# Four of the last ten stores in three parts of 112, 8 and 8 rows

## The chip, the core and the metric

The kernel runs on one core of one Trainium2 chip. The metric is the device time of one execution in microseconds, and the number for a kernel is the median of several executions. Times inside an execution come from a hardware profile of one further execution; they count from its first instruction.

The engines of the core are named as the profile names them: PE (TensorE, matmul), PEld (its weight loads), DVE (VectorE), ACT (ScalarE), POOL (GpSimd) and SP (SyncE). Sixteen DMA engines move data between the device's memory (DRAM) and the on-chip memory (SBUF, 128 partitions, called rows here). A DMA instruction on SP's or POOL's queue only starts a transfer; the DMA engines carry it out.

## What is computed

An input of 8 sequences, 3264 positions and 192 channels first passes a depthwise convolution over the last seven positions with softmax weights for each of 8 heads. The result x then passes a spectral mix: its lowest 64 Fourier modes along the sequence are multiplied by one complex 192 x 192 matrix for each mode, transformed back and added, and a last product with a relu follows.

```python
x = attn_out                        # the convolution's result
X = np.fft.rfft(x, axis=1)
Xr, Xi = (np.real(X[:, :n_modes]), np.imag(X[:, :n_modes]))
Yr = np.einsum('bmd,mde->bme', Xr, w_r) - np.einsum('bmd,mde->bme', Xi, w_i)
Yi = np.einsum('bmd,mde->bme', Xr, w_i) + np.einsum('bmd,mde->bme', Xi, w_r)
Y[:, :n_modes] = Yr + 1j * Yi
y = np.fft.irfft(Y, n=S, axis=1)
u = x + y
return (u + np.maximum(u @ w_ch, 0.0)).astype(np.float32)
```

The output is float32 in DRAM, 8 x 3264 x 192, 20 MB.

## The kernel before

The kernel works in two long stages. In the first (to about 97 us) POOL's queue loads x and the mode matrices, and PE convolves, transforms and mixes. In the second (from about 105 us to the end) the output is computed and stored, item by item. This second stage is what the change touches.

**Items.** The 8 sequences are taken as four pairs (NQ = 4, index q). A sequence is cut into 13 blocks of 256 positions (NB = 13), the last one of 192. One item is one block of one pair: the list `duos` (line 669) has N = 52 of them, n = 0 to 51. Partition p of an item holds two neighbouring positions (index a) of each of the two sequences (index i), so an item is 128 partitions x 2 x 2 x 192 float32 values, 384 KB. Items 12, 25, 38 and 51 are the short last blocks of a pair: they have 96 partitions (PL) and 288 KB.

**The computation of an item.** For each a, PE forms the sum in one bank of its accumulator memory with `product` (line 722) and `full` (line 702), ACT applies the relu in place (`clamp`, line 695), and `add` (line 673) lets DVE add x and write the result to an output buffer in SBUF (line 684). Only the very last half item is copied by ACT (line 682), after PE has added x with the identity matrix (line 803). There are NO = 6 output buffers, called arena in the profile; item n uses buffer n % 6.

**The stores.** After the second half (a = 1) of an item, `add` starts one DMA on SP's queue that writes the whole item to DRAM (line 690). The first three items are stored in two halves. For each partition the DMA moves two runs, one for each sequence of the pair; each run is 2 x 192 float32 values, 1536 bytes. A store of 128 rows is thus 256 packets of 1536 bytes, and one of 96 rows 192. There are 55 stores in all, and SP does nothing else in this stage. SP issues them in the order of the items: before each it waits for DVE's result, and, in an EVENT_SEMAPHORE instruction of the same line, for the completion of an earlier DMA, since the stores take turns on eight completion semaphores. At the end (line 896) SP waits for all of them.

**The order of the work around it.** The loop at line 839 runs over the half items k and mixes the products of neighbouring half items by hand, so that PE always has something to do; the last six half items (TAIL) have an order of their own. The change leaves all of this as it is.

Of the kernel before, what the change touches and what calls it, by code (L numbers as in the profile page):

```python
# [20 lines left out]
def kernel(  # L21
# [9 lines left out]
    nc = tc.nc  # L31
    B, S, D = x.shape
# [5 lines left out]
    P = 128  # L38
# [120 lines left out]
    def load_part(q, b0, n):  # L159
# [6 lines left out]
        if nf < n:  # L166
# [6 lines left out]
                                           ap=[[0, P], [KK, H], [1, KK]]))  # L173
# [64 lines left out]
    for h0 in (0, H // 2):  # L238
        hs = slice(h0, h0 + H // 2)
        for lag in range(KK):  # L240
            k = lag // 2
            nc.vector.copy_predicated(
                out=pk4[:, hs, lag % 2, :],
                mask=masks[:, PW * k:PW * (k + 1)].unsqueeze(1).to_broadcast([P, H // 2, PW]),
                data=ta3[:, hs, KK - 1 - lag:KK - lag].to_broadcast([P, H // 2, PW]))
        for g in range(4):
            c0 = 1 + 32 * (g % 2)
            dst, srcv = band[32 * g:32 * g + 32, hs, :, c0:c0 + PW], pk4[32 * g:32 * g + 32, hs, :, :]
# [421 lines left out]
    N = len(duos)  # L670
    place = {}

    def add(bank, n, a):

        o = outs[n % NO]
        q, t = duos[n][0]
        pn = PL if t == NT - 2 else P
        s = NT * q + t
        srcv = bank[0:pn, 0:2 * D].rearrange("p (i d) -> p i d", i=2)
        if (n, a) == (N - 1, 1):  # L680

            nc.scalar.copy(out=o[0:pn, :, a, :], in_=srcv)  # L682
        else:
            nc.vector.tensor_tensor(out=o[0:pn, :, a, :], in0=srcv, in1=xall[0:pn, s + a, :, :], op=ALU.add)  # L684
        apart = n < 3
        if apart or a == 1:
            a0, w = (a, 1) if apart else (0, 2)
            dst = bass.AP(tensor=out.tensor, offset=out.offset + (2 * q * S + P * t + a0) * D,
                          ap=[[2 * D, pn], [S * D, 2], [1, w * D]])
            nc.sync.dma_start(out=dst, in_=o[0:pn, :, a0:a0 + w, :].rearrange("p i a d -> p i (a d)"))  # L690

    def clamp(bank, on_scalar=True):
        z = bank[:, 0:2 * D]
# [57 lines left out]
    d = ND - 2  # L751
# [12 lines left out]
    d = ND - 1  # L764
# [25 lines left out]
    def upper_y(k):  # L790
        if 0 <= k < K - 2:
            turn([end[k, 0]])
            product(k, 1, pieces(k, 1, "y")[0], False, True)
            add(bank[k], *items[k])

    def lower_y(k):
        if 0 <= k < K - 2:
            product(k, 0, pieces(k, 0, "y")[0], False, False)
        elif K - 2 <= k < K:
            n, a = items[k]  # L800
            if k == K - 1:
                qt = NT * duos[n][0][0] + duos[n][0][1] + a
                nc.tensor.matmul(bank[k][:, 0:2 * D], ident[:], xall[:, qt, :, :].rearrange("p i d -> p (i d)"),  # L803
                                 start=False, stop=False, skip_group_check=True)
            full(n, "y", a)
            add(bank[k], n, a)
# [10 lines left out]
    for n in range(2):  # L817
        whole(n, "y")
        for a in range(2):
            add(place[n][a], n, a)  # L820
# [80 lines left out]
```

## Time and profile before

| what | value |
|---|---|
| median of 3 runs | 171.35 us (171.32 to 171.36) |
| time of the profiled execution | 171.73 us |
| its span, from the first to the last instruction | 169.9 us (169.87) |
| granted TensorE clock, mean | 0.999 |
| stores: DMA issues on SP of line 690 | 55 |
| bytes written to DRAM | 20.05 MB |
| DMA queue q1 (SP's), packets | 14848 |
| DMA queue q8 (instruction), packets and bytes | 20, 0.33 MB |

The span is what the engines' instructions cover; the time of an execution also has what lies around it, 1.9 us here. Busy time says how long an engine worked, in total; the 40 slices show when. A slice of this span is 4.25 us. The views used below are the page (busy times, slices, DMA issues), the chain of waits that ended last, stages (a row gives the stage, then for PE, PEld, DVE, ACT and POOL the busy time with the number of instructions, then the granted PE clock, the busy share of the DMA engines and GB/s), and the instructions of one line (duration as min/median/max in ns, first and last start). The trace also lists every DMA packet with its start, duration and size, and the time of each completion, but not the DMA engine that carried it.

### The profile page before, as it was taken

The page shows a single profiled execution, that of the slowest core. Times are in us where ns is not written, and L with a number is a line of the kernel's source. Part 1 is how long each engine was busy: PE and PEld are TensorE (multiplying, and loading weights), DVE is VectorE, ACT ScalarE, POOL GpSimd, SP SyncE. Part 2 cuts the span into 40 slices and gives each one's busy share as a digit, 9 for nine tenths or more (in the row PEclk, how much of TensorE's full clock was granted, in tenths as well). Part 3 has the DMA queues.
Part 4 walks back from the last instruction along what each step waited for, and adds up shares of the span by engine and source line. Part 5 has one row for each costly group of instructions (what it writes and reads, how often), then busy time and mean ns, then how long its engine had stood idle before and what let it go on. Part 6 is the DMA issues. An engine that isn't in the chain of part 4 may idle for free.

```text
span 169.9 us, 6328 instructions
## 1 busy us (share of the span) xinstructions
PE 159.1 (94%) x2643; PEld 126.9 (75%) x2643; DVE 125.2 (74%) x245; ACT 109.9 (65%) x209; POOL 38.7 (23%) x71
## 2 busy tenths in 40 slices
PE   6997789999999999999999998999999999999980
PEld 6983666776565655579999865899999999999940
DVE  4899554684572845748778644899999999999990
ACT  8485870653572735636776753788888888887770
POOL 7941763341521712002620000600000000000000
PEclk9999999999999999999999999999999999999999
DMA  2999999999999999999999970589899999999995
GB/s 26 193 202 204 204 204 204 203 204 203 202 204 204 207 208 208 208 207 208 211 203 208 209 126 4 170 310 357 305 350 359 346 320 344 351 326 340 339 387 173
DMA packets 37180, 40.09 MB, mean 236 GB/s; under 512 B 1984, under 2 KB 37152, under 8 KB 37152
## 3 DMA queue, kind: packets, MB, share of 16 engines
q0 software_dynamic: 22304, 19.61, 71.9%
q1 hardware_dynamic: 14848, 20.09, 32.4%
q8 instruction: 20, 0.33, 0.8%
q14 instruction: 8, 0.07, 0.1%
HBM read 39.10 MB, written 20.05 MB: 348 GB/s over the span
## 4 chain that ended last, share of the span: by engine, by line
DMA 58%; PE 36%; issue 1%; POOL 1%; ACT 1%; POOLq 0%; ACTq 0%
PE z L722 34%; DMA xall<-in_x_dram 25%; DMA arena<-in_moe_w_i_dram 18%; DMA ct<-in_moe_w_i_dram 14%; POOL xall L165 1%; PE z L702 1%; PE z L643 0%; PE z L551 0%; ACT z L695 0%; ACT arena L682 0%; PE z L634 0%; ACT shared L569 0%; PE z L644 0%; PE z L575 0%; PE z L803 0%
## 5 line engine op out<-in xcount | busy, mean ns | idle before, releaser
L684 DVE TENSOR_TENSOR arena<-z,xall 128x384 f32<-128x384 f32 (+1 forms) x103 | 56.7, 557 | 2.1 <-PE z L722 0.6
L695 ACT ACTIVATE z<-z 128x384 f32<-128x384 f32 x102 | 48.0, 475 | 11.1 <-PE z L722 2.7
L722 PE MATMUL z<-wm,ct 64*128 64x192 bf16 x200 | 47.4, 243 | 0.0
L722 PE MATMUL z<-arena,ftab 64*128 64x384 bf16 x308 | 44.5, 322 | 0.0
L722 PEld LDWEIGHTS <-ct 64*128 64x128 bf16 x600 | 38.5, 94 | 4.7 <-issue 0.3
L317 PE MATMUL z<-xall,shared 64*64 64x480 bf16 (+3 forms) x768 | 38.5, 338 | 2.2 <-DMA xall<-in_x_dram 1.5
L317 PEld LDWEIGHTS <-shared 64*64 64x64 bf16 x768 | 25.1, 106 | 13.3 <-DMA xall<-in_x_dram 1.6
L722 PE MATMUL z<-wsw,ct 64*128 64x192 bf16 x300 | 34.0, 243 | 0.0
L722 PEld LDWEIGHTS <-ftab 64*128 64x128 bf16 x396 | 33.4, 94 | 0.6 <-issue 0.3
L361 DVE CAST xall<-z 128x480 bf16<-128x480 f32 (+1 forms) x32 | 20.6, 645 | 12.7 <-PE z L317 11.7
L359 ACT CAST xall<-z 128x480 bf16<-128x480 f32 (+1 forms) x32 | 17.5, 548 | 15.2 <-PE z L317 15.2
L722 PE MATMUL z<-w,ct 64*128 64x192 bf16 x100 | 24.3, 243 | 0.0
L416 DVE COPY ct<-z 128x1024 bf16<-128x1024 bf16 x27 | 18.4, 687 | 5.2 <-PE z L419 4.5
L419 PE MATMUL z<-ident,xall 128*128 128x128 bf16 x312 | 20.0, 219 | 0.0
L419 PEld LDWEIGHTS <-xall 128*128 128x128 bf16 x312 | 17.7, 98 | 1.9 <-issue 1.1
L378 PE MATMUL z<-xall,ftab 128*128 128x384 bf16 (+3 forms) x114 | 18.0, 312 | 0.2 <-DVE xall L361 0.2
L165 POOL DMA_DIRECT2D xall<-in_x_dram x16 | 14.2, 894 | 12.8 <-DMA xall<-in_x_dram 11.9
L378 PEld LDWEIGHTS <-ftab 128*128 128x128 bf16 (+1 forms) x114 | 10.2, 98 | 7.6 <-issue 1.5
L414 ACT COPY ct<-z 128x1024 bf16<-128x1024 bf16 x12 | 12.1, 1012 | 4.1 <-PE z L419 4.1
L722 PE MATMUL z<-mixa,ftab 64*128 64x384 bf16 x88 | 13.4, 323 | 0.0
L196 PE MATMUL z<-xall 128*128 128x144 bf16 x92 | 7.9, 264 | 1.6 <-DVE xall L183 1.6
L296 POOL DMA_DIRECT2D arena<-in_moe_w_r_dram x7 | 4.6, 652 | 20.6 <-PE z L551 14.5
(116 smaller groups left out, 140.6 us busy)
## 6 DMA issues: line engine op xcount, KB each, us to landing
out_dram<-arena SPq DMA_DIRECT2D x45, 384.0 KB, 3.5
xall<-in_x_dram POOLq DMA_DIRECT2D x4, 864.0 KB, 17.4
xall<-in_x_dram POOLq DMA_DIRECT2D x4, 576.0 KB, 18.7
arena<-in_moe_w_r_dram POOLq DMA_DIRECT2D x3, 576.0 KB, 15.0
arena<-in_moe_w_i_dram POOLq DMA_DIRECT2D x3, 576.0 KB, 14.8
ct<-in_moe_w_r_dram POOLq DMA_DIRECT2D x3, 576.0 KB, 20.6
ct<-in_moe_w_i_dram POOLq DMA_DIRECT2D x3, 576.0 KB, 23.6
xall<-in_x_dram POOLq DMA_DIRECT2D x2, 672.0 KB, 11.4
```

Source lines behind the costliest of these rows:

```text
L165: nc.gpsimd.dma_start(out=xin[:, s0:s0 + nf, 2 * D * i:2 * D * (i + 1)], in_=src)
L196: nc.tensor.matmul(free[3][:, 0, 0:144], zeros[:, 0:P], zeros[:, 0:144], start=True, stop=True, skip_group_check=True)
L317: yield nc.tensor.matmul(o, band[r, h, int(a != a1), c0:c0 + 64], xin5[r, s1:s1 + n, :, a1, dsl], start=(row == 0 and a1 == 0), stop=(row ...
L359: nc.scalar.copy(out=dst[:, a], in_=srcv)
L361: nc.vector.tensor_copy(out=dst[:, a], in_=srcv)
L378: nc.tensor.matmul(xp[:, :, ds], ftab[0:k, t, :], xall[0:k, NT * q + t, :, ds], start=(j == 0), stop=(j == len(work) - 1), skip_group_chec ...
L414: nc.scalar.copy(out=out, in_=in_)
L416: nc.vector.tensor_copy(out=out, in_=in_)
L419: nc.tensor.matmul(o, in_, ident[:], start=True, stop=True, is_transpose=True)
L684: nc.vector.tensor_tensor(out=o[0:pn, :, a, :], in0=srcv, in1=xall[0:pn, s + a, :, :], op=ALU.add)
L695: nc.scalar.activation(out=z, in_=z, func=ACT.Relu)
L722: mm = nc.tensor.matmul(target(bank[k], cols, r), l, r, start=first, stop=last, skip_group_check=True)
```

## The change

The stores of items N - 10, N - 8, N - 6 and N - 4, which are items 42, 44, 46 and 48, go in three DMAs instead of one: rows 0 to 111, rows 112 to 119 and rows 120 to 127. The bytes, their place in DRAM and the moment at which `add` starts them stay the same. All other items are stored in one DMA, as before.

```diff
+    PARTS, UNEVEN = (P - 16, 8, 8), (N - 10, N - 8, N - 6, N - 4)
+
     def add(bank, n, a):
...
         if apart or a == 1:
             a0, w = (a, 1) if apart else (0, 2)
-            dst = bass.AP(tensor=out.tensor, offset=out.offset + (2 * q * S + P * t + a0) * D,
-                          ap=[[2 * D, pn], [S * D, 2], [1, w * D]])
-            nc.sync.dma_start(out=dst, in_=o[0:pn, :, a0:a0 + w, :].rearrange("p i a d -> p i (a d)"))
+            p0 = 0
+            for rows in PARTS if n in UNEVEN else (pn,):
+                dst = bass.AP(tensor=out.tensor, offset=out.offset + (2 * q * S + P * t + a0 + 2 * p0) * D,
+                              ap=[[2 * D, rows], [S * D, 2], [1, w * D]])
+                nc.sync.dma_start(out=dst, in_=o[p0:p0 + rows, :, a0:a0 + w, :].rearrange("p i a d -> p i (a d)"))
+                p0 += rows
```

## The prediction

> **What bounds the kernel now.** I read the page first, for which engine is full where.
>
> ```profile
> PE 159.1 (94%) x2643; PEld 126.9 (75%) x2643; DVE 125.2 (74%) x245; ACT 109.9 (65%) x209; POOL 38.7 (23%) x71
> ...
> DMA  2999999999999999999999970589899999999995
> GB/s 26 193 202 204 204 204 204 203 204 203 202 204 204 207 208 208 208 207 208 211 203 208 209 126 4 170 310 357 305 350 359 346 320 344 351 326 340 339 387 173
> ```
>
> The last 60 us pair a PE that is full with DMA engines that are nearly full (310 to 387 GB/s, all of it the stores). Second, the chain of waits, for where compute ends.
>
> ```profile
> 164.63 0.32 PE z L803
> 164.96 0.18 PE z L702
> 165.13 0.02 issue
> 165.16 0.47 ACT arena L682
> ```
>
> Compute ends at 165.63, the span at 169.87. The 4.2 us between belong to stores alone, so third, the stages around the end.
>
> ```profile
> 152.40:153.40 1.00, 1.00 (x22) 0.96 (x20) 0.97 (x3) 0.90 (x2) 0.00 (x0) 1.00 0.94 270
> 155.00:156.00 1.00, 1.00 (x22) 0.92 (x20) 0.97 (x2) 0.81 (x3) 0.00 (x0) 1.00 0.94 350
> 161.00:162.00 1.00, 1.00 (x22) 0.85 (x19) 1.00 (x3) 0.77 (x3) 0.00 (x0) 1.00 1.04 389
> ...
> 166.80:167.50 0.70, 0.00 (x0) 0.00 (x0) 0.00 (x0) 0.00 (x0) 0.00 (x0) 1.00 1.00 290
> 168.00:168.60 0.60, 0.00 (x0) 0.00 (x0) 0.00 (x0) 0.00 (x0) 0.00 (x0) 1.00 0.06 23
> ```
>
> The last two numbers are the DMA share of 16 engines and GB/s. From 168.00 to 168.60 the share is 0.06, one engine of sixteen: 23 GB/s over 0.6 us is 14 KB, nine pieces of 1536 B. Fifteen engines are done, one is late by about 0.6 us, and the end waits for it. The trace's list of packets says the same: the latest engine's last packet ends at 168.60, the next one's at 167.98, and 1.27 us after 168.60 the span ends (landing, SP's last wait, the closing drains). That engine has been late since about 113 us. The page's queue q8 (instruction, 20 packets, 0.33 MB) explains it if they all pass through one engine: 0.8% of 16 spans of 169.9 us over 20 is 1.1 us each. A late engine works through a store in 0.97 us (landings of successive stores) and gets one each 1.145 us, so it recovers slowly.
>
> The second thing in these rows is the time of a packet: share x 16 us over the number of packets. At 155 it is 0.94 x 16 / (350,000/1536) = 66 ns, at 161 also 66. At 152.4 and 166.8, where the trace moves a 96-row store, it is 86 and 85 ns. A 96-row store gives an engine 12 packets instead of 16 and yet is hardly faster:
>
> ```profile
> out_dram<-arena SPq DMA_DIRECT2D x45, 384.0 KB, 3.5
> ...
> out_dram<-arena SPq DMA_DIRECT2D x4, 288.0 KB, 3.4
> ```
>
> [...]
>
> Fourth, SP, which issues every store.
>
> ```profile
> L690 SPq DMA_DIRECT2D out_dram<-arena x55: 334/372/769, 107.2 to 165.7; - x55
> L690 SPq EVENT_SEMAPHORE  x52: 17/17/727, 96.7 to 165.3; - x52
> ...
> DMA to landing us min/median/max: 2.0/3.4/4.4
> ```
>
> **The change, part by part.** Items 42, 44, 46 and 48 are touched (N is 52), issued at 156.09, 158.37, 160.66 and 162.62. No byte is added: 256 packets become 224 + 16 + 16.
>
> Issues: 8 more on SP. The nearest back-to-back issues, items 0 and 1, stand 0.46 to 0.49 us apart. Three take 1.4 us, so a plain store behind them goes 0.3 us late (1.145 us between items), and the pair of an uneven and a plain item takes 1.9 us of the 2.0 to 2.3 between pairs. Items 50 and 51 go at 164.88 and 165.66 as before; cost 0, covered by the empty half of SP's time. At the longest issue in the trace (0.77) a pair would take 3.1 us and the last store would go 2.7 us late (third rival).
>
> Semaphores: a store takes over the semaphore of the DMA eight before and SP waits for that one's landing (the x52 row). With three parts, eight DMAs are about four items: item 51 at 165.66 waits for item 47, which landed at 165.29; item 50 at 164.88 for 46, landed 164.28; 49 for 45, 48 for 44, 47 for 43 have 0.3 to 0.4 us. Behind such a wait stand only later stores, and DVE, which refills a buffer six items later (6.9 us against a landing of at most 4.4). If landings slip 1.5 us, the last store goes 1.1 us late, at 166.8, starts 0.9 later and would end the span near 169.8; not the bound if the sum below is larger.
>
> The part of 112 rows: 14 packets per engine, if it is dealt over sixteen like 128 (16 each) and 96 (12 each). Bounds: 61 ns each (packets of 65 ns start 61 apart), 0.86 us; at the 94 ns of the worst half microsecond of a 96-row store, 1.32. I take 85 ns, the mean in these windows: 1.19 us, where the whole store took 0.98.
>
> The parts of 8 rows: 16 packets each. Nothing in the trace is that narrow. A row is two packets, and the wide stores give an engine whole rows, so I take eight engines with two packets each. Low bound: no sharing, 0.12 us a part. [...]
>
> [...]
>
> Sum on an engine that gets both small parts: 1.19 + 2 x 0.43 = 2.05 for an uneven store, 0.98 for a plain one, 3.03 a pair, 12.12 for four pairs. The store of item 42 starts 0.86 after its issue (first packets of an idle engine), 156.95; four pairs end at 169.07; item 50 adds 0.98, item 51 twelve packets at 70 ns, 0.85: 170.9. With 1.27 behind it the span ends at 172.2, against 169.87: **+2.3 us**. At the low bounds (0.86 and 0.12) a pair takes 2.08, less than the time between items, nothing piles up, and the late engine sets the end (first rival). At the high bounds a pair takes 3.28; the span ends at 173.3, +3.5. [...]
>
> The profiled execution shows 169.87 of span in a time of 171.73; the runs' median is 171.35. The difference goes on top of the median: **173.6**.
>
> **Rivals.** First, *relief*: packets stay at 61 to 65 ns and the late engine is one of the eight spared. It loses two packets in each uneven store, 8 x 61 ns = 0.49 us. The other eight gain 8 packets and 8 closing writes, 0.55 us, and have 0.6 us before they are the last. 171.35 - 0.49 = **170.9**, faster. For it: one engine alone is late, and moving eight of its packets is the right size. Against it: the packets of the 96-row store. It decides as long as an uneven store costs the loaded engines under about 1.2 us. [...]
>
> Second, *wrong half*: the same packet times, the late engine among the loaded eight: + 0.55, **171.9**. For it: the trace names no engine.
>
> Third, *SP too slow*: each issue nearer 0.77 than 0.46; the last store goes at 168.36, starts 0.9 later, takes 0.74, and 1.27 behind it the span ends at 171.3, **172.8**. Against: 334 to 377 ns in nearly every row.
>
> Fourth, *no effect*: relief and sharing cancel, or all sixteen engines take one packet of each small part and keep 16: **171.35**.
>
> **How the numbers follow.** Sharing 0.57 at 173.6; relief 0.25 at 170.9; wrong half 0.08 at 171.9; SP 0.04 at 172.8; no effect 0.06. This kernel's measurement tells 0.2% (0.34 us) from no change. Faster 0.25, all of it relief. Same 0.06. Slower 0.69. The likeliest's own range is 171.9 (small parts at half the sharing, a pair in 2.60) to 175.4 (high bounds, plain stores slowed too). The range reaches down to relief: 170.8 to 175.4, with 0.15 outside.
>
> **What would show it.** Sharing: the time per packet in windows from 157 to 165 above 75 ns where it was 66, about half of the engines at work in the last 2 us (share 0.3 to 0.5) where one was, landings of items 48 to 51 later by over 1 us, SP waits on out_dram in the middle of the tail. Relief: 65 ns throughout and the tail of one engine at 168.0 gone. Wrong half: that tail grows to 1.1 us at share 0.06. SP: issues of items 50 and 51 later with short waits. I am wrong above all if rows 112 to 127 can be read by eight engines at once at full rate.

## The result and the profile after

The changed kernel takes 173.63 us (median of 6 runs, 173.03 to 174.85) against 171.36 us before (6 runs, 170.92 to 171.71): a ratio of 1.014, with a 95% interval of 1.0104 to 1.0176. It is slower by 2.3 us, and the forecast was 173.6. The profiled execution took 173.37 us, so its trace shows 1.6 of these 2.3 us. The ratios with their intervals, here and below, can differ by up to a quarter of a percent from the quotient of the two medians.

First the page, the busy engines and the last rows of its slices; a slice is 4.29 us here.

```profile
PE 160.8 (94%) x2643; PEld 127.6 (74%) x2643; DVE 125.5 (73%) x245; ACT 109.8 (64%) x209; POOL 39.2 (23%) x71
...
DMA  2999999999999999999999940789899999989995
GB/s 26 204 203 204 207 201 203 204 203 203 202 204 205 207 208 208 208 207 208 211 203 208 209 71 6 245 317 352 287 378 348 345 318 344 360 317 323 307 315 174
```

The DMA row is as full as before, but the last five slices move 317, 323, 307, 315 and 174 GB/s where they moved 326, 340, 339, 387 and 173. The computation is not what got longer. The chain of waits, which does not follow the last stores, ends as before at 165.64 (the row gives start, length and what):

```profile
107.06 56.98 PE z L727 x973
164.12 0.48 ACT z L700
165.17 0.47 ACT arena L684
```

From there to the end it is 5.8 us instead of 4.2. The stages of the tail (columns as before: stage, busy times, PE clock, DMA share, GB/s):

```profile
155.00:156.00 1.00, 1.00 (x23) 0.92 (x20) 0.97 (x2) 0.81 (x3) 0.00 (x0) 1.00 0.93 349
...
162.00:163.00 1.00, 1.00 (x22) 0.79 (x19) 1.00 (x3) 0.78 (x3) 0.00 (x0) 1.00 1.02 307
163.00:164.00 1.00, 1.00 (x15) 0.60 (x9) 0.97 (x3) 0.90 (x2) 0.00 (x0) 1.00 0.68 221
...
167.00:168.00 1.00, 0.00 (x0) 0.00 (x0) 0.00 (x0) 0.00 (x0) 0.00 (x0) 0.76 1.06 396
168.00:169.00 1.00, 0.00 (x0) 0.00 (x0) 0.00 (x0) 0.00 (x0) 0.00 (x0) 0.50 1.01 315
169.00:170.00 1.00, 0.00 (x0) 0.00 (x0) 0.00 (x0) 0.00 (x0) 0.00 (x0) 0.50 0.28 92
```

The same two microseconds before:

```profile
162.00:163.00 1.00, 1.00 (x22) 0.79 (x18) 1.00 (x3) 0.78 (x3) 0.00 (x0) 1.00 1.02 381
163.00:164.00 1.00, 1.00 (x15) 0.59 (x9) 0.97 (x3) 0.90 (x2) 0.00 (x0) 1.00 1.07 398
```

Two losses can be read here. The time of a packet is share x 16 us over the number of packets: 1.02 x 16 / (307,000/1536) = 82 ns at 162 where it was 66, while 155 and 167, where 128-row stores go alone, still have 65 to 66. (The 79 ns at 168 are no part of the loss: that is the 96-row store of item 51, which had 85 ns before too.) And at 163 the share is 0.68: a third of the DMA engines' time is empty although PE and DVE deliver as before. The half PE clock at the end is granted after PE's last matmul and costs nothing.

The nine microseconds from 157 to 166 in one row each, before and after:

```profile
157.00:166.00 9.00, 7.96 (x121) 6.07 (x118) 8.14 (x16) 6.56 (x14) 0.00 (x0) 1.00 0.97 359
```

```profile
157.00:166.00 9.00, 7.96 (x121) 6.08 (x118) 8.15 (x16) 6.56 (x14) 0.00 (x0) 1.00 0.91 303
```

The compute engines did the same in them; the stores moved 56 GB/s less, over 9 us 0.5 MB, 1.3 stores of a whole item. At 0.98 us a store that is 1.3 us, most of the 1.6 us that this execution is longer. Of the loss, packets account for more than idleness: 66 ns became 74 (12%), the share fell from 0.97 to 0.91 (6%).

The empty time at 163 follows a long issue on SP. The issues of the stores, and one of them:

```profile
L694 SPq DMA_DIRECT2D out_dram<-arena x63: 335/372/1200, 107.2 to 166.3; - x63
L694 SPq EVENT_SEMAPHORE  x52: 17/17/728, 96.1 to 166.2; - x52
```

```profile
161.63 1.20 SPq L694 DMA_DIRECT2D out_dram<-arena  x1
```

This is the third part of item 46. SP sits in it for 1.20 us, so item 47 goes at 162.93 instead of 161.69, and the DMA engines run dry at 163. The third part of item 48 takes 0.80, and the first part of item 44 takes 0.83 where its store took 0.69 before. The last store goes at 166.26, 0.61 us late, and the span ends 5.2 us behind it instead of 4.2: the 1.6 us are 0.6 of a later last issue and 1.0 of stores that finish later behind it. SP did not wait for a landing in this stretch; its only waits there are for DVE:

```profile
SPq L694 <- DVE arena L686: 2.7, 5, 1.1
```

### The profile page after: what moved, and what is told of

It reads as the page before. It is cut to its first block, busy times and chain, and to the rows that moved or that the text cites. A ratio compares the mean times of both kernels' runs of the same rounds, so it can differ in the third digit from the quotient of the medians.

```text
span 171.4 us, 6338 instructions
## 1 busy us (share of the span) xinstructions
PE 160.8 (94%) x2643; PEld 127.6 (74%) x2643; DVE 125.5 (73%) x245; ACT 109.8 (64%) x209; POOL 39.2 (23%) x71
## 4 chain that ended last, share of the span: by engine, by line
PE 92%; issue 2%; DVE 2%; ACT 1%; DVEq 0%; ACTq 0%
PE z L727 34%; PE z L317 22%; PE z L419 12%; PE z L378 11%; PE z L196 5%; PE z L551 3%; PE z L652 1%; PE z L396 1%; PE z L707 1%; PE z L634 1%; DVE ct L416 1%; PE z L455 1%; DVE xall L361 0%; PE z L643 0%; ACT z L700 0%
## 5 line engine op out<-in xcount | busy, mean ns | idle before, releaser
L378 PE MATMUL z<-xall,ftab 128*128 128x384 bf16 (+3 forms) x114 | 19.0, 323 | 0.2 <-DVE xall L361 0.2
L196 PE MATMUL z<-xall 128*128 128x144 bf16 x92 | 8.5, 276 | 1.6 <-DVE xall L183 1.6
L381 ACT COPY ct<-z 128x384 f32<-128x384 f32 x4 | 1.9, 478 | 12.3 <-PE z L378 12.3
```

What stands on the lines that cost most here:

```text
L196: nc.tensor.matmul(free[3][:, 0, 0:144], zeros[:, 0:P], zeros[:, 0:144], start=True, stop=True, skip_group_check=True)
L378: nc.tensor.matmul(xp[:, :, ds], ftab[0:k, t, :], xall[0:k, NT * q + t, :, ds], start=(j == 0), stop=(j == len(work) - 1), skip_group_chec ...
```

## The experiments

Each kernel differs from the changed one, and is compared with the kernel before on the same chip. The excerpts show the lines that decide; where a loop is replaced, the address and slice lines that follow it change with it and are left out. Two theories stand against each other. The sharing theory is the prediction's main outcome: packets of a store that does not span all 128 rows take longer, as those of the 96-row store did before (85 ns against 66), and stores of 128 rows keep their 65 to 66. The issue theory: more issues on SP delay the later stores, whatever their rows.

**Three wide parts.** SP issues as often as in the change, but each DMA spans all 128 rows.

```diff
-            for rows in PARTS if n in UNEVEN else (pn,):
+            cuts = ((0, 1, 0, 2), (1, 1, 0, 1), (1, 1, 1, 1)) if n in UNEVEN else ((0, 2, a0, w),)
+            for i0, ni, b0, nb in cuts:
```

> The same four items are stored in three DMAs each, but every DMA keeps all 128 rows (one sequence whole, the other in two halves of 768 bytes a row), so SP issues as often as in the changed kernel and no DMA is narrow. [...] Issue theory (three issues on SP delay the later stores and leave the DMA engines idle): the last store goes about 0.6 us late as in the changed kernel, some issues take 0.8 to 1.2 us, time 172.5 to 173.6.

Measured: 172.17 us, ratio 1.003 (1.0014 to 1.0045). The stage from 159 to 166 moves 366 GB/s at a share of 1.01.

```profile
159.00:166.00 7.00, 5.36 (x75) 3.64 (x70) 5.62 (x11) 4.49 (x10) 0.00 (x0) 1.00 1.01 366
```

In the trace's packet list those of 1536 bytes take 65 ns in this stage, as before. One issue, at 156.39, took 2.18 us beside an instruction packet of 8 KB on queue q14; the others of these items took 0.35 to 0.46. Three issues for each of four items cost 0.5 us by the ratio and 0.8 by the medians, a fifth to a third of the change's loss. That is less than the issue theory wanted, and stores of all 128 rows kept their packet time, as the sharing theory has it.

**Only the 112 rows.** The small parts are left out.

```diff
-    PARTS, UNEVEN = (P - 16, 8, 8), (N - 10, N - 8, N - 6, N - 4)
+    PARTS, UNEVEN = (P - 16,), (N - 10, N - 8, N - 6, N - 4)
```

> Rows 112 to 127 of the four items are not stored at all, so each is one DMA of 112 rows; SP issues as often as in the kernel before and 6% fewer bytes go in these items. Sharing theory: packets of the 112-row stores take about 85 ns, 1.19 us a store, so the saved packets gain nothing: 171.0 to 171.7. Issue theory: packets at 65 ns, the late engine has 8 packets fewer, 0.49 us: 170.7 to 171.0.

Measured: 171.8 us, ratio 1.0024 (1.001 to 1.0039).

```profile
157.00:166.00 9.00, 7.29 (x111) 5.44 (x105) 7.48 (x15) 6.21 (x14) 0.00 (x0) 1.00 0.94 323
```

With SP as free as before (its last store is not late) and 192 KB less to move (an eighth of these items, not the 6% of the expectation), the kernel is not faster but a little slower: 0.94 x 16 / (323,000/1536) = 72 ns a packet in a stretch that also holds 128-row stores. If these keep 65, the 112-row packets took about 78, an estimate from this row, which makes 1.10 us a store. By this estimate a store of 112 rows costs more than the one of 128 that it replaces (0.98). The time lies just above both ranges.

**112 and 16 rows.**

```diff
+    PARTS, UNEVEN = (P - 16, 16), (N - 10, N - 8, N - 6, N - 4)
```

> The four items go in two DMAs, of 112 and of 16 rows. Issue theory: a pair of items needs 1.4 us of SP's 2.0 to 2.3, no later store is late, time 171.2 to 171.6. Sharing theory: 1.19 us for the 112 rows and 0.25 to 0.43 for the 16 adjacent ones, 1.5 to 1.6 against 0.98 per uneven store, time 172.2 to 173.2, though SP is not late by itself.

Measured: 173.2 us, ratio 1.0109 (1.0086 to 1.0132), at the upper edge of what the sharing theory said. One more DMA for each item and none over eight engines, since the 16 rows complete on sixteen. Still the loss is over three quarters of the change's. SP is late here too: plain stores behind the 16 rows have issues of 0.60 to 1.19 us, and the last store goes 0.5 us late.

**The small parts on POOL's queue.**

```diff
-                nc.sync.dma_start(out=dst, in_=...)
+                (nc.gpsimd if rows == 8 else nc.sync).dma_start(out=dst, in_=...)
```

> The parts are those of the changed kernel, 112, 8 and 8 rows, but POOL's queue, which has nothing else to do then, starts the two small ones. SP issues as often as before. Issue theory: back to the time before or under it, 170.8 to 171.5, no issue on SP over 0.5 us. Sharing theory: as slow as the changed kernel, 172.5 to 174, with packets at 75 to 85 ns in the last 12 us, and the small parts' packets, which now show on POOL's queue, well over 65 ns.

Measured: 173.88 us, ratio 1.0149 (1.0125 to 1.0173): nothing is gained by taking the extra issues off SP, and SP's own stores get long issues all the same.

```profile
157.00:166.00 9.00, 8.07 (x123) 6.15 (x119) 8.25 (x16) 6.62 (x15) 3.84 (x8) 1.00 0.93 295
```

```profile
L694 SPq DMA_DIRECT2D out_dram<-arena x55: 334/372/1407, 107.3 to 166.5; - x55
```

The issue of 1.41 us is item 50's, a plain store at 164.99. So the long issues need no extra issue ahead of them on SP's queue; here they come while the DMA engines are behind, and that the backlog causes them is not shown. SP was not made free by this: its last store goes 0.7 us late. On POOL's queue the small parts' packets can be told from the others: 64 of 3072 bytes, 34 of which took 119 to 121 ns, about twice the 65 of half their size, while 25 took 195 to 434. These parts are not quite the change's, though: the packets are twice as long, and each part completes in sixteen updates.

**Adjacent and strided rows.** A pair of kernels asks whether it matters that the eight rows are neighbours. Both use parts of 96, 8 and 8 rows and leave 16 rows out.

```diff
+            for p0, step, rows in ((0, 1, 96), (96, 1, 8), (104, 1, 8)) if n in UNEVEN else ((0, 1, pn),):
...
+            for p0, step, rows in ((0, 1, 96), (96, 4, 8), (97, 4, 8)) if n in UNEVEN else ((0, 1, pn),):
```

> The four items go in parts of 96, 8 and 8 rows; the small ones are rows 96 to 103 and 104 to 111, adjacent rows as in the changed kernel, and rows 112 to 127 are not stored. Sharing theory: 12 packets at 85 ns and twice 0.43 us, 1.88 us per uneven store, a pair 2.86 of the 2.0 to 2.3 between pairs: 172.2 to 173.4. Its rival says that narrow DMAs cost by their number and their few engines, whichever rows they take: the same time as e6_strided, within 0.3%.

> As e5_adjacent, with the same number of DMAs, rows and bytes, but the two small parts take every fourth row, 96, 100, ... 124 and 97, 101, ... 125; the other 16 rows above 95 are not stored. [...] Rival: the same time as e5_adjacent within 0.3%.

Measured: 173.74 us, ratio 1.0144 (1.0122 to 1.0166), adjacent; 173.92 us, ratio 1.0154 (1.0132 to 1.0176), strided. The strided rows cost what the adjacent ones cost, within the rival's 0.3%; the adjacent ones lie 0.3 us above the sharing theory's range. The pair is not clean, though: SP needs 0.67 to 0.95 us to issue a strided part against 0.30 to 0.64 for six of the eight adjacent ones, and with 2.2 to 2.6 us of issues for a pair of items SP itself is too slow there: the last store goes 1.8 us late, in the adjacent profile 1.4. In the completions there is what could be a trace of a difference: the eight engines of item 42's parts, while there is no backlog, land within 0.32 and 0.41 us of each other when the rows are adjacent, and seven of the eight within 0.10 and 0.04 us when they are strided. But the strided parts were issued more slowly, and all of their landings come after those of the 96 rows (all but one engine by 157.89, the first strided landing at 157.91), while the adjacent parts begin to land among them. The tighter landings may be no more than that.

**The same question with two DMAs,** so that SP has time: 96 and 16 rows.

```diff
+            for p0, step, rows in ((0, 1, 96), (96, 1, 16)) if n in UNEVEN else ((0, 1, pn),):
...
+            for p0, step, rows in ((0, 1, 96), (96, 2, 16)) if n in UNEVEN else ((0, 1, pn),):
```

> The four items go in two DMAs, rows 0 to 95 and the 16 adjacent rows 96 to 111; rows 112 to 127 are not stored. Two issues fit SP's time even at the 0.7 us that a strided narrow DMA took in e6_strided, so that SP does not bound this pair of runs. Sharing theory: 1.02 us for the 96 rows and up to 0.43 for the 16, a pair 2.2 to 2.4: 171.6 to 172.8, slower than e10_strided16 by 0.3 us or more. Rival (a narrow DMA costs by its number): equal to e10_strided16 within 0.3 us.

> As e9_adjacent16, but the 16 rows of the second DMA are every second one, 96, 98, ... 126, and the 16 others above 95 but for these are not stored. [...] Rival: equal within 0.3 us.

Measured: 173.48 us, ratio 1.0114 (1.0077 to 1.015), adjacent; 173.6 us, ratio 1.0105 (1.0071 to 1.0139), strided. No difference shows, but each interval is 0.6 us wide to either side, so the 0.3 us that was to decide cannot be seen. The adjacent rows are slower than the 172.8 that was expected at most, and the strided ones are no faster, although an eighth of the bytes of these items is missing. The expectation that SP would not bound the pair did not hold either: in the strided profile the last store goes 10.2 us after item 42's first part, in the adjacent one 9.6, as before. The two profiles are of unlike executions, the slowest of the strided kernel (174.3) and the fastest of the adjacent one (172.07), so their rows do not compare the shapes. Whether neighbouring rows cost more than strided ones is therefore left open by these four kernels.

**Two halves.** No narrow part, no DMA over fewer than sixteen engines, nothing left out.

```diff
+    PARTS, UNEVEN = (64, 64), (N - 10, N - 8, N - 6, N - 4)
```

> The four items go in two DMAs of 64 rows each, 0 to 63 and 64 to 127; everything is stored, an engine gets eight packets of each, and SP issues once more per item, in rows next to each other. [...] Rival (the cost comes from parts that go over eight engines, or from the number of DMAs): 171.2 to 172.0, as e1_three_wide, packets at 65 ns.

Measured: 173.42 us, ratio 1.0129 (1.0102 to 1.0156), nearly the whole loss of the change.

```profile
160.00:161.00 1.00, 1.00 (x22) 0.82 (x20) 0.98 (x3) 0.83 (x2) 0.00 (x0) 1.00 1.00 278
161.00:162.00 1.00, 1.00 (x22) 0.85 (x19) 1.00 (x4) 0.81 (x3) 0.00 (x0) 1.00 1.01 300
```

All engines are at work and move 278 and 300 GB/s instead of 389: 88 and 83 ns a packet, where the rival had 65 and the kernel before 66. Against the three wide parts, with more DMAs and 366 GB/s, this is the cleanest pair of the study: what costs here is that a store has 64 rows instead of 128. SP is not free of blame here either:

```profile
L694 SPq DMA_DIRECT2D out_dram<-arena x59: 334/372/1677, 106.6 to 166.1; - x59
```

A 64-row issue takes 0.6 us or more, and the last store goes 1.1 us late, against 0.8 in the kernel of the three wide parts. These 0.3 us are far less than the 1.4 us between what the two lose by the medians.

**The change earlier.**

```diff
+    PARTS, UNEVEN = (P - 16, 8, 8), (N - 28, N - 26, N - 24, N - 22)
```

> The change as it is, 112, 8 and 8 rows, but on items 24, 26, 28 and 30 instead of 42, 44, 46 and 48. If the cost is a backlog of the DMA engines, as the prediction's sum has it, the twenty plain stores behind (0.98 us of work in 1.145 us each) take it in, over 2.5 us of slack: 171.0 to 172.0. If the parts cost a fixed time wherever they are: 173.0 to 173.8.

Measured: 171.52 us, ratio 1.0007 (0.9994 to 1.0019). The same twelve DMAs, and no loss. The stages show the slow packets (76 ns from 137 to 142) and that they are over by the end (67 ns):

```profile
137.00:142.00 5.00, 5.00 (x92) 4.66 (x89) 4.87 (x10) 4.13 (x10) 0.00 (x0) 1.00 0.88 283
142.00:148.00 6.00, 6.00 (x108) 5.59 (x106) 5.85 (x11) 4.99 (x11) 0.00 (x0) 1.00 0.96 335
157.00:166.00 9.00, 7.55 (x114) 5.67 (x109) 7.75 (x15) 6.49 (x14) 0.00 (x0) 1.00 0.95 349
```

So the cost is a backlog, which the later stores work off in the 0.16 us that each leaves free.

**Item 48 alone.**

```diff
+    PARTS, UNEVEN = (P - 16, 8, 8), (N - 4,)
```

> The change as it is, on item 48 alone. The prediction's sum: the loaded engines finish item 48 at 165.5 instead of 164.5, items 49 to 51 follow back to back and end at 168.3, before the late engine's 168.5 to 168.6; no cost, 171.1 to 171.6. If each uneven item costs its share of the change's 2.3 us wherever it stands: 171.9 or more.

Measured: 172.01 us, ratio 1.0039 (1.0017 to 1.0061), over a quarter of the whole loss from one item, where the sum saw none. Its one profile suggests why. The late engine lands last in all three parts, at 165.24, 165.45 and 165.66, so it is one of the eight that carry the small parts, and each adds 0.21 us to its work. In the profile of the changed kernel it was not one of them: item 42's 112 rows land last 4.38 us after their issue, at 160.48, its small parts completely by 159.02 and 159.42.

**One item in 120 and 8 rows.**

```diff
+    PARTS, UNEVEN = (P - 8, 8), (N - 9,)
```

> One item alone, 43, goes in two DMAs of 120 and 8 rows. [...]

Measured: 171.88 us, ratio 1.0027 (1.0009 to 1.0045). The 120 rows complete on fifteen engines, one fewer than 128 rows. Left out of this item, the late engine would have 16 packets less to move, 0.98 us at the 61 ns from one packet's start to the next before. But it is among the fifteen (landing 4.16 us after the issue, at 161.12) and, by the times, also in the small part (161.36, when the seven others had landed by 160.42). It was spared nothing. Its distance from the others does shrink, from 1.95 us at item 42 to 0.78 at item 44, but because the others are later. The small part's issue took 1.45 us, beside a q14 packet again, so this run does not price 120 rows alone.

No version here beats the kernel before; the nearest, the earlier change, equals it.

**Late or not, over all profiles.** Before the change the last store goes 9.57 us after item 42's first issue. So it does in the profiles of the 112 rows alone, the 16 adjacent rows, the earlier change, item 48 alone and the 120 rows, and these executions took 0.1 to 0.8 us more than the median before. In the change and the other seven kernels it goes 0.5 to 1.8 us late. Of these eight, seven took 1.8 to 2.9 us more; the three wide parts, with a last store 0.8 us late and packets at 65 ns, took only 0.8 more. So a late SP adds about its lateness, narrower stores add something of their own, and every loss over 1 us has both in its profile.

## Why the prediction was right

The time came out as forecast, 173.63 against 173.6, and so did the main cause, the slower packets of stores that do not span all rows; most terms of the sum, and the way in which the loss spreads, did not. That the figure was met to 0.03 us is luck: two terms were about twice too large, and they made up for held issues that had no term.

**What bounds the kernel: right.** The stores set the end, and a loss in them counts in full while compute ends at the same 165.6.

**The 112 rows at 85 ns, 1.19 us instead of 0.98: right in kind, about half in size.** The kernel with these parts alone is 0.24% slower in spite of fewer bytes, 0.4 us where 4 x 0.21 = 0.8 us was priced, and the estimate of 78 ns from its row gives 1.10. The late engine, which has no empty time in the tail, would then lose 4 x 0.12 = 0.5 us; that it is this engine that costs the 0.4 is argued, not shown. That other widths than 128 rows are slower, as the 96-row stores are (85 ns), held for 112 rows (the estimate of 78) and for 64 (83 to 88).

**The small parts at 0.43 us each: too high.** The change against its 112 rows alone is 1.4% - 0.24%, 2.0 us for eight small parts, 0.25 us each with the held issues in it. The landings say about 0.2: the third parts of items 44 and 48 land 0.18 to 0.22 us after the second, engine by engine in order of landing. Both values lie above the low bound of 0.12. No run shows the 0.43 that the sum uses, nor the 0.49 that its pair of 3.28 at the high bounds contains; the runs showed these 0.2 to 0.25 in their place. That eight rows cost more for being neighbours found no support in the total times: strided rows cost the same (1.0154 against 1.0144), though SP hides what they may have gained, and the tighter landings of the strided item 42 have another possible reason. Why the packets of a narrower store take longer is not shown either: the traces give the time of a packet, not what it waits for.

**What the sum gives with these sizes.** An uneven store takes 1.10 + 2 x 0.2 = 1.50 us and a pair 2.48, and the span would end at 156.95 + 9.92 + 0.98 + 0.85 + 1.27 = 169.97, only 0.1 us later than before. So the sum's path, a backlog of these two terms, does not make up the loss by itself.

**Extra issues at nothing: wrong by a little by themselves, by more through the backlog.** Three wide parts cost 0.3%. The long issues of 0.80 to 1.20 us had no term in the sum; the last store went 0.61 us late, where the sum had 0 and the third rival 2.7. That 2.7 counts three of the four pairs: at 0.77 us an issue, sixteen issues from 156.09 on put item 50 at 168.4, 3.5 us late, and the rival's time comes to 173 or more, so the total alone could not tell it from the forecast. Its cause, eight more issues on SP that are long by themselves, falls with the three wide parts, which have as many and cost 0.5 to 0.8 us. With the small parts on POOL the time stayed the same too, but SP's own stores were late there as well.

**The signs: two of four.** The landings of items 48 to 51 are 1.1 to 1.6 us later, as said. Packets took 82 ns at 162 and 74 over the nine microseconds, about the 75 that was set. Waits for landings in the middle of the tail did not appear; the hold-up sits inside the issues. Half of the engines at work at the end did not appear either.

**Eight loaded engines and half of them at work at the end: wrong.** At 168 to 169 the share is 1.01, then 0.28 for the next microsecond. All sixteen were late. The 112-row part goes over all of them, and when SP is held up in an issue, the eight spared engines get no new store either. The sum had put 0.86 of the 1.07 us that it added for an uneven store on eight engines; the runs put less there and the rest, in part as held issues, on all sixteen.

**Backlog that plain stores work off: right,** and tested by the change at items 24 to 30. By the same rule the late engine should have hidden item 48 alone; it did not, and in the one profile of that kernel the late engine is itself loaded. Which it was in the other executions is not recorded.

**Relief and wrong half.** Both rivals fall as the main outcome. Their premise of one fixed late engine falls too: in the profiles of the changed kernel, of the adjacent and strided parts and of the earlier change it lay on the spared side; in those of the 120 rows and of item 48 alone on the loaded one. In the trace before, the lag of the last engine to land is down to 0.10 us for the store issued at 140.0 and back at 1.73 for the one issued at 142.3, which was under way at the next 16 KB packet of queue q8 (143.72, 0.95 us); it jumps likewise at those of 113.40 and 157.08. So, as far as the times tell, such a packet makes an engine late anew, and it need not be the same one. How many engines a store goes over is read from its completions: 16 updates for 128, 112, 96, 64 and 16 rows, 15 for 120 behind an early one, and for 8 rows one update 0.1 to 0.2 us behind the issue (in the changed kernel) and eight later ones. So an engine got whole rows there: the 16 packets of 8 rows went over eight engines, not sixteen. Which of the sixteen engines these eight are cannot be seen in these traces.

What stays open: whether neighbouring rows cost more than strided ones, since the strided kernels were bound by SP as well; what slows the packets of a narrower store; how the loss divides between slower packets and held issues, which come together in every large loss; and what exactly holds an issue on SP for up to 1.4 us when the DMA engines are behind.

## What to carry to other kernels

Balancing bytes between DMA engines is worth little if the new shape makes the bytes slower: compare the time per packet, share x engines over packets, between the shapes that the trace already holds, here 85 ns for 96 rows against 66 for 128, before counting packets. At the end of this kernel, where nothing is left to work off a backlog, no other division of the stores was faster than one DMA over all partitions. And before aiming at the one engine that is late, see in several profiles that it is always the same.

## What the runs showed of the hardware

A DMA issue on SP was not of constant length: before, the median of the 55 is 0.37 us, and the last, of 96 rows, took 0.34; in the kernel of the two halves 64 rows took 0.6 or more, and eight strided rows took 0.67 to 0.95. The longest issue was 0.77 before, 1.20 in the change (at 161.63), 1.41 with the small parts on POOL (a plain store at 164.99, with the DMA engines behind and no wait shown), 1.68 with the two halves and 2.18 with the three wide parts, beside a q14 instruction packet. Stores of 64 adjacent rows moved 278 and 300 GB/s with all engines at work (two halves, from 160 to 162); stores of 128 rows moved 389 (before, from 161 to 162).
